# The output projection of a fused convolution and SiLU kernel: from 32-column products to a 20-product scheme of 64 columns

## The chip, the cores and the metric

The kernel runs on one core of a Trainium2 chip. The metric is device time in microseconds (us); lower is better. Engines are named as in the profile: PE is TensorE's matmuls, PEld its weight loads, DVE is VectorE, ACT is ScalarE, POOL is GpSimd, and SP issues transfers.

## The reference

A causal convolution of 7 taps over 8 sequences of 4096 tokens with 192 channels, with softmax weights by head, is followed by a two-layer network with SiLU. Everything is 32 bit.

```python
w = softmax(weight)                       # 8 heads x 7 taps
out[b, s, c] = sum_k w[head(c), k] * x_pad[b, s + k, c]
x = out.reshape(32768, 192)
h = x @ w_in                              # 192 -> 2048
g = h * (1.0 / (1.0 + np.exp(-h)))
y = g @ w_out                             # 2048 -> 192
```

## The kernel before, in words

The 32768 tokens go in 32 blocks of 1024, each as two halves (n = 0, 1) of TB = 512 tokens. Channels stand on partitions in the whole kernel. A block passes these stages:

- `load` brings x in, `turn_in` turns it (DVE), `halo_in` adds the six tokens before the block. `conv` makes 18 steps (3 channel parts x 7 taps, the first without a sum): ScalarE multiplies by the tap, and from block 4 on a POOL-issued transfer adds the product to `nat` in SBUF; before that DVE does both. `spread` copies the result into both partition halves of `dup` (SP), and `win` forms sums of it (DVE).
- Up-projection: 2048 inner channels are done in five groups of chunks, each with a scheme of 15 products (`product`, steps P0 to P14) instead of 18, and six plain ones (`plain`, steps L). Each contracts over 64 rows, so two of them fit the 128 rows of the array side by side. `sums_h` (steps u, X, a, b) combines them in PSUM and SBUF, on ScalarE and DVE, and its steps S apply SiLU into `g`.
- Output projection: `sum_g` (steps t) forms four sums of `g` for each of NJ = 4 chunk elements on DVE. `out_slot` (steps D0 to D5) multiplies them with 32 columns of weights at a time, four products next to each other in the 128 columns of the array; `wx` holds sums of weights made once by `combine_out` on POOL. `merge` (steps x, y, z on ScalarE, M on DVE) brings the parts together, `turn_out` (o) turns them back, and `store_out` (st) sends them out from SP.

The order of all engines is written by hand: `PLAN` is a list of such steps for one turn of the loop, and `pin` keeps each engine's instructions in that order. A sign tells which block a step is for: none for block b of the turn, "-" for the block before, "=" two before, "+" for the next. PSUM has eight banks (one `[128, 512]` tile each), and tables (`CHAIN_BANKS`, `XBANKS`, `PLAIN_BANKS`, `ACC`) say which bank each step uses. `tc` derives the waits between engines from what each instruction reads and writes. Block 0 runs without the schemes (`up_plain`, `down_plain`), `START` is the hand-made order for block 0's output and for blocks 1 and 2, and `finish` one for the last block's output.

Of the kernel before, what the change touches and what calls it, by code (L numbers as in the profile page):

```python
# [17 lines left out]
def kernel(  # L18
# [53 lines left out]
    gpool = ctx.enter_context(tc.tile_pool(name="gp", bufs=2 * NJ))  # L72
# [9 lines left out]
        "+ld.1 -P0.2 -u1.2 -X4.2 -P7.2 -P11.2 -S4.2 =o.2 =st.2 -a1.1 -S1.1 -P0.3 -P12.2 -X4.3 "  # L82
        "-P7.3 v.01 -P11.3 -P12.3 -a5.2 -P4.2 -P14.2 -S4.3 -u1.3 -b1.2 -P10.2 -a5.3 -P8.1 -S5.0 "
        "-S1.0 -a1.2 -S3.2 -P4.3 v.10 -P8.2 -P14.3 -S3.3 -b1.3 -a1.3 -P10.3 P5.4 -S5.1 v.11 "
        "-P8.3 P5.0 v.02 -D1.00 =st.3 -t.00 -b5.3 -a0.2 -a0.3 -sp.2 -D1.30 u5.4 -a0.1 -D1.01 "
        "v.22 v.12 -D0.00 -S0.3 v.23 -D0.31 -D1.10 -t.01 -t.03 -D2.00 -sp.0 -b5.2 -t.02 -D4.01 "
        "-S1.2 -S5.2 -D5.00 -D2.01 v.03 -D5.01 -D3.00 -S0.1 -t.10 -D1.20 -D4.00 v.13 v.24 "
        "-D3.01 -t.11 -D2.11 -D2.10 -t.13 -D5.11 v.14 -D4.10 v.04 -D0.21 -S1.3 -w.0 -w.1 -S0.2 "
        "v.25 -t.20 -S5.4 -t.21 -D5.10 -D4.11 +ld.2 -D1.21 -D0.30 -D0.11 -t.23 -S5.3 -D4.20 "
        "-D5.20 -t.12 -D3.10 -D3.11 -D2.21 -D2.20 -D0.20 -D4.21 -t.22 -D3.21 v.05 -D1.31 -D5.21 "  # L90
        "-t.30 -D0.01 -w.2 -t.31 -t.33 -D5.31 -D1.11 v.15 v.26 +i.2 u5.0 -D0.10 -z1.0 -t.32 "
        "-y0.0 v.06 -D5.30 -x2.3 -x2.0 -D3.30 -w.3 -w.4 -y1.0 -D2.31 -D2.30 -M1.0 -D3.31 -y2.0 "
        "-x2.1 -w.5 -x2.2 -D3.20 -x0.0 -D4.31 -D4.30 -M6.0 -M2.0 L.00 v.16 -M3.0 -M4.0 P2.0 "
        "u4.0 P5.1 +i.1 L.10 u5.1 L.02 -M5.0 -o.3 -x1.0 P3.0 P6.0 u2.0 X2.0 P2.4 u4.4 -o.0 L.01 "
        "SL.0 L.12 L.11 SL.1 +ld.0 P1.0 u0.0 SL.2 P9.0 P6.4 u2.4 P13.0 S2.0 X4.0 -M7.0 -st.0 "
        "+i.0 P2.1 P3.4 X2.4 u4.1 P0.0 u1.0 P7.0 a5.0 P12.0 P11.0 S4.0 b1.0 P1.4 u0.4 P9.4 X4.4 "
        "P4.0 P13.4 a1.0 P14.0 P10.0 b5.0 P7.4 a5.4 P0.4 S2.4 +ha.0 +v.00 S3.0 P6.1 P8.0 P3.1 "
        "u1.4 u2.1 P11.4 a0.0 X2.1 P12.4 P4.4 a1.4 +v.20 b1.4 S4.4 S0.0 +v.21 P5.2 u5.2 P14.4 "
        "S3.4 P1.1 u0.1 P13.1 S2.1 P8.4 a0.4 P5.3 u5.3 sp.1 P2.2 P9.1 X4.1 u4.2 P10.4 -o.1 P0.1 "
        "P2.3 P12.1 u1.1 P7.1 b5.4 u4.3 P11.1 S4.1 P6.2 -st.1 b1.1 u2.2 P3.2 P6.3 P10.1 S1.4 "  # L100
        "a5.1 P3.3 u2.3 P14.1 S3.1 X2.2 P1.2 P13.2 S2.2 P9.2 u0.2 P4.1 b5.1 X2.3 P13.3 P1.3 "
        "u0.3 P9.3 S2.3 S0.4"
    )
    START = (
        "-ld.1 =v.10 -ld.0 =v.00 =v.11 =v.12 =dp.0 =dp.1 =dp.2 =dp.3 =v.13 =v.20 =v.21 =v.22 "
        "=v.23 =v.24 =v.25 =dp.4 =dp.5 =v.14 =dp.6 =dp.7 =dp.8 =dp.9 =v.15 =v.16 -ld.2 =sp.1 "
        "=dp.10 =dp.11 =v.26 =v.01 =v.02 =v.03 =dp.12 =v.04 =dp.13 =v.05 =v.06 =dp.14 =dp.15 "
        "=dp.16 =sp.2 =dp.17 =dp.18 =dp.19 =dp.20 =sp.0 -i.2 =go.2 -i.1 =dp.21 =dp.22 =dp.23 "
        "=dp.24 -i.0 =dp.25 =dp.26 =dp.27 =dp.28 =dp.29 =dp.30 -ha.0 =dp.31 =dp.32 =dp.33 "
        "=dp.34 ld.1 =w.0 =w.1 =dp.35 =dp.36 -v.00 =dp.37 =dp.38 =w.2 =dp.39 =dp.40 =dp.41 "  # L110
        "-v.01 =dp.42 -v.20 =dp.43 =dp.44 -v.02 -v.03 -v.10 -v.11 -v.12 =dp.45 =cp.0 =dp.46 "
        "=dp.47 =cp.1 -v.21 -P5.0 =w.3 -P5.4 -L.00 -u5.0 -v.13 -v.14 -L.11 -v.22 -P2.0 =cp.2 "
        "-u5.4 -P2.4 -L.12 -P3.0 -u4.0 -u4.4 -P6.0 -L.02 -u2.0 -L.01 -SL.0 -L.10 -SL.1 -P6.4 "
        "-u2.4 -P3.4 -SL.2 =o.1 -v.15 -P1.0 -u0.0 -X2.0 -P13.0 -S2.0 -v.23 -P5.2 =w.4 -u5.2 "
        "-P9.0 -P1.4 -u0.4 -P0.0 -u1.0 -P12.0 -P2.2 -X2.4 -P0.4 -P13.4 -S2.4 -X4.0 -P7.0 -u1.4 "
        "=o.2 -P14.0 -b1.0 -P10.0 =w.5 -S3.0 -u4.2 -a5.0 -b5.0 -S5.0 -v.04 -P11.0 -P9.4 -X4.4 "
        "-P14.4 =o.0 -P4.0 -S4.0 -a1.0 -P6.2 -u2.2 -P5.1 -P12.4 -b1.4 -P11.4 -P7.4 -P3.2 -P1.2 "
        "-P8.0 -u5.1 -S4.4 -a5.4 -P10.4 -u0.2 -S3.4 -P2.1 -u4.1 -P4.4 =st.0 -X2.2 -P13.2 -S2.2 "
        "-P9.2 -P0.2 -u1.2 -a0.0 -b5.4 -S5.4 -a1.4 -P12.2 -v.16 -P6.1 -u2.1 =st.1 -P5.3 -u5.3 "
        "-P8.4 -P14.2 -X4.2 -S3.2 i.1 -a0.4 -b1.2 -P3.1 -X2.1 -P1.1 -P7.2 -u0.1 -a5.2 -P2.3 "  # L120
        "-u4.3 -P3.3 -P11.2 -v.24 -P9.1 -S4.2 -X4.1 -P13.1 -P4.2 -P6.3 -S2.1 -a1.2 -u2.3 -P10.2 "
        "-b5.2 -P0.1 -P7.1 -P8.2 -P11.1 -X2.3 -P1.3 -S1.0 -P9.3 -v.25 -u1.1 -P14.1 -S4.1 -P12.1 "
        "-u0.3 -S1.4 -P13.3 -S3.1 -a5.1 -P4.1 -X4.3 -P7.3 -P0.3 -a0.2 -S5.2 -sp.1 +ld.1 -P12.3 "
        "P5.4 -v.26 -P11.3 -b1.1 -a5.3 -a1.1 -u1.3 -P10.1 -b1.3 -S2.3 -P4.3 -a1.3 -v.05 =st.2 "
        "-P8.1 -b5.1 -P10.3 -sp.2 -S0.4 -P14.3 -P8.3 ld.0 -S4.3 -S1.1 P5.0 -a0.1 -S0.0 -t.00 "
        "-D1.31 -D1.11 -S0.2 -D1.01 -S3.3 -D1.30 -t.01 -D2.00 -D2.01 -b5.3 -S5.3 -S1.2 -S5.1 "
        "-D0.11 -t.03 -D4.00 -a0.3 -D4.01 -t.02 -D3.00 u5.4 -D0.20 -S0.1 ld.2 -D5.00 -t.10 "
        "-t.11 -D2.11 -D3.01 -v.06 -sp.0 -D1.20 -S0.3 -D5.01 -t.13 -D4.11 -D5.10 -D4.10 i.2 "
        "-S1.3 i.0 -t.12 -D5.11 -D3.11 -t.20 ha.0 -t.21 -D0.10 -D2.10 u5.0 -D2.21 -w.0 -D2.20 "
        "-w.1 v.20 -D3.10 -D0.00 v.00 -t.23 -D4.21 -D4.20 -w.2 v.01 -t.22 -D3.21 -D0.21 -D0.30 "  # L130
        "-D0.31 -w.3 -t.30 v.21 -t.31 -D1.10 v.02 v.22 -D0.01 -D2.31 -t.32 -t.33 -D1.21 v.10 "
        "-D5.30 v.23 v.24 -y0.0 -D1.00 -y1.0 -D5.31 -z1.0 -D5.20 -D5.21 -x2.0 -x2.2 v.11 -D3.31 "
        "-D2.30 -x2.1 v.03 -x2.3 P2.0 u4.0 P3.0 -w.5 L.02 P2.4 u4.4 v.12 v.13 v.14 P6.0 u2.0 "
        "v.15 v.25 v.26 v.04 -M1.0 -M2.0 -y2.0 L.00 +ld.0 -M6.0 L.01 SL.0 X2.0 P6.4 u2.4 -D4.30 "
        "-D3.20 -D3.30 -M3.0 -x0.0 -D4.31 -x1.0 P9.0 P1.0 u0.0 -o.0 P13.0 S2.0 X4.0 P1.4 u0.4 "
        "-M4.0 -M5.0 P3.4 P5.1 u5.1 P11.0 X2.4 -w.4 P7.0 S4.0 P0.0 P12.0 P2.1 u1.0 P9.4 P0.4 "
        "u1.4 P13.4 a5.0 P4.0 b1.0 P10.0 X4.4 u4.1 S2.4 P7.4 P11.4 S4.4 P14.4 S3.4 v.16 P6.1 "
        "u2.1 P14.0 v.05 L.10 a1.0 a5.4 +ld.2 b5.0 P8.0 +i.2 a0.0 S3.0 P3.1 P4.4 a1.4 L.11 L.12 "
        "SL.1 P5.2 P12.4 SL.2 X2.1 v.06 P8.4 -st.0 u5.2 P1.1 P13.1 u0.1 b1.4 P5.3 sp.1 S0.0 "
        "u5.3 -o.3 S2.1 P12.1 P2.2 u4.2 -M7.0 P9.1 P0.1 u1.1 S1.4 +i.1 P2.3 u4.3 +i.0 a0.4 X4.1 "  # L140
        "S0.4 P10.4 P6.2 u2.2 P3.2 P7.1 P14.1 S3.1 P11.1 b1.1 b5.4 +ha.0 P10.1 +v.20 S4.1 P3.3 "
        "-o.1 P6.3 u2.3 X2.2 P9.2 P1.2 u0.2 a5.1 P4.1 X2.3 +v.21 P13.2 S2.2 P13.3 S2.3 P1.3 "
        "u0.3 -st.1 +v.00 P9.3 b5.1"
# [3 lines left out]
        ((4, 1, 2, 7, 7), (3, 4, 6, 5, 5), (1, 3, 3, 1, 0)),  # L147
        ((0, 2, 5, 4, 6), (1, 6, 1, 0, 7), (5, 3, 2, 3, 0)),
        ((5, 2, 5, 6, 7), (0, 4, 0, 3, 3), (1, 7, 2, 1, 1)),
    )  # L150
    XBANKS = (
        ((6, 2, 4, 2, 0), (6, 0, 0, 0, 4)),
        ((5, 1, 2, 7, 3), (4, 7, 3, 7, 4)),
        ((4, 0, 1, 7, 4), (6, 3, 1, 7, 6)),
    )
    PLAIN_BANKS = (
        (0, 2, 1),
        (5, 3, 4),
        (6, 3, 1),
    )  # L160
    ACC = (
        (1, 2, 7, 4, 3, 5, 7),
        (3, 4, 6, 1, 0, 2, 7),
        (0, 6, 1, 3, 4, 2, 7),
    )
# [91 lines left out]
    WC = 2 * NK * P  # L257
    in32 = moe_w_in.bitcast(I32).rearrange("(k r) (a m c) -> r k a m c", r=R, a=2, m=NM)
    out32 = moe_w_out.bitcast(I32).rearrange("(a q e p) d -> a q p e d", a=2, e=2, p=P)
    wr = [const.tile([P, 2, NK, P], F32, name=f"wr{j}") for j in range(NJ)]  # L260
    ws = [const.tile([P, 2, NK, P], F32, name=f"ws{j}") for j in range(NJ)]
    wo = [const.tile([P, 2, 2, D], F32, name=f"wo{j}") for j in range(NJ)]
    wx = [const.tile([P, 3, 2, HD], F32, name=f"wx{j}") for j in range(NJ)]
    raws = {}

    def raw_tile(key):

        pool, tag = (gpool, "g") if key in (("i", 2), ("i", 3)) else (tpool, "t")
        raws[key] = pool.tile([P, 4 * TB], I32, tag=tag, name="raw")[:, 0 : 2 * WC]
        return raws[key]  # L270
# [611 lines left out]
    def step(b, token):  # L882
# [49 lines left out]
        if b == NB - 1 and token == closing:  # L932
            for t in later:
                step(b, t)
# [201 lines left out]
```

## Time and profile before

| | |
|---|---|
| median of 3 runs | 2319.7 us (2319.48 to 2320.31) |
| profiled execution, span | 2317.9 us |
| PE busy | 2310.2 us (100%) |
| DVE, ACT, POOL busy | 1797.9 (78%), 1496.0 (65%), 534.9 (23%) us |
| output products, `out_slot` (L765) | share of the chain that ended last: 45% |
| up-projection, `product` (L649) and `plain` (L666) | 39% and 5% |
| granted TensorE clock | 1.000 |

The page gives each engine's busy time, and the chain of work that ended last, followed back from the end: at each step to what released it. A 32-bit matmul is listed as two records. "128*32" behind a matmul is the part of the array that it uses, rows by columns. A group's line has its count, its busy time, the mean duration of one, and the idle time of the engine ahead of it with what ended it. The span is the profiled execution's own time from the first to the last instruction; the runs' times are some 2 us longer.

### The profile page before, as it was taken

The page shows a single profiled execution, that of the slowest core. Times are in us where ns is not written, and L with a number is a line of the kernel's source. Part 1 is how long each engine was busy: PE and PEld are TensorE (multiplying, and loading weights), DVE is VectorE, ACT ScalarE, POOL GpSimd, SP SyncE. Part 2 cuts the span into 40 slices and gives each one's busy share as a digit, 9 for nine tenths or more (in the row PEclk, how much of TensorE's full clock was granted, in tenths as well). Part 3 has the DMA queues.
Part 4 walks back from the last instruction along what each step waited for, and adds up shares of the span by engine and source line. Part 5 has one row for each costly group of instructions (what it writes and reads, how often), then busy time and mean ns, then how long its engine had stood idle before and what let it go on. Part 6 is the DMA issues. An engine that isn't in the chain of part 4 may idle for free.

```text
span 2317.9 us, 45421 instructions
## 1 busy us (share of the span) xinstructions
PE 2310.2 (100%) x17630; PEld 949.6 (41%) x17630; DVE 1797.9 (78%) x2373; ACT 1496.0 (65%) x2779; POOL 534.9 (23%) x675
## 2 busy tenths in 40 slices
PE   9999999999999999999999999999999999999999
PEld 5454443444433344433444334443334443344433
DVE  8998777777777777777777777777777777777777
ACT  5347766677666686666776667866667666677543
POOL 4921112221122211222211222112221212221100
PEclk9999999999999999999999999999999999999999
DMA  7236557766567765677655676556776557765401
GB/s 159 58 62 101 98 100 118 123 115 102 95 113 120 121 105 93 109 120 121 110 98 99 115 124 117 102 93 113 119 123 108 94 104 120 120 114 93 81 17 25
DMA packets 522601, 238.81 MB, mean 103 GB/s; under 512 B 430368, under 2 KB 435488, under 8 KB 522384
## 3 DMA queue, kind: packets, MB, share of 16 engines
q0 software_dynamic: 73120, 133.89, 34.4%
q1 hardware_dynamic: 447392, 101.78, 25.0%
q8 instruction: 138, 2.26, 0.4%
q14 instruction: 79, 0.65, 0.1%
q10 hardware_dynamic: 1872, 0.23, 0.1%
HBM read 31.46 MB, written 25.17 MB: 24 GB/s over the span
## 4 chain that ended last, share of the span: by engine, by line
PE 89%; DVE 0%; issue 0%; ACT 0%; ACTq 0%
PE ps L765 45%; PE ps L649 39%; PE ps L666 5%; DVE cmb L175 0%; ACT u L175 0%; DVE osb L175 0%; ACTq L175 0%
## 5 line engine op out<-in xcount | busy, mean ns | idle before, releaser
L512 POOL DMA_DIRECT2D nat<-u x504 | 432.6, 947 | 1544.6 <-ACT u L511 1192.3
L765 PE MATMUL ps<-g,wo 128*32 128x512 f32 x2976 | 694.9, 592 | 0.0
L649 PE MATMUL ps<-win,wr 64*128 64x512 f32 x1550 | 688.7, 591 | 0.8 <-ACT yx L828 0.8
L649 PE MATMUL ps<-win,ws 64*128 64x512 f32 x1550 | 644.3, 589 | 0.0
L698 ACT COPY u<-ps 128x512 f32<-128x512 f32 x775 | 452.2, 587 | 166.8 <-PE ps L649 93.8
L765 PE MATMUL ps<-t,wo 128*32 128x512 f32 (+2 forms) x4528 | 538.5, 446 | 0.0
L765 PE MATMUL ps<-t,wx 128*32 128x512 f32 x2976 | 485.1, 592 | 0.0
L649 PE MATMUL ps<-dup,wr 64*128 64x512 f32 x868 | 425.6, 589 | 0.0
L511 ACT ACTIVATE u<-xt,taps 128x512 f32<-128x512 f32 x504 | 346.0, 715 | 44.0 <-DMA nat<-u 43.6
L733 DVE TENSOR_TENSOR t<-g,t 128x1024 f32<-128x1024 f32 x248 | 303.3, 1223 | 89.7 <-PE ps L765 84.2
L692 DVE TENSOR_TENSOR g<-u,ps 128x512 f32<-128x512 f32 x465 | 312.2, 682 | 72.2 <-PE ps L649 58.8
L649 PEld LDWEIGHTS ps<-win,wr 64*128 64x128 f32 x1550 | 275.7, 187 | 217.1 <-issue 177.1
L733 DVE TENSOR_TENSOR t<-g 128x1024 f32<-128x1024 f32 x248 | 298.8, 1216 | 76.4 <-PE ps L765 56.7
L692 DVE TENSOR_TENSOR ps<-u,ps 128x512 f32<-128x512 f32 x310 | 215.7, 696 | 132.3 <-PE ps L649 62.0
L710 ACT ACTIVATE g<-ps 128x512 f32<-128x512 f32 x465 | 281.0, 604 | 48.6 <-PE ps L649 47.0
L649 PEld LDWEIGHTS ps<-win,ws 64*128 64x128 f32 x1550 | 258.8, 187 | 126.1 <-issue 103.9
L710 ACT ACTIVATE g<-g 128x512 f32<-128x512 f32 x465 | 281.4, 629 | 30.3 <-DVE g L692 30.3
L765 PEld LDWEIGHTS ps<-t,wo 128*32 128x32 f32 x4528 | 181.4, 110 | 239.2 <-issue 227.6
L649 PE MATMUL ps<-dup,ws 64*128 64x512 f32 x682 | 271.9, 589 | 0.0
L831 ACT COPY cmb<-ps 96x512 f32<-96x512 f32 x30 | 17.4, 581 | 393.1 <-PE ps L765 393.1
L765 PE MATMUL ps<-g,wx 128*32 128x512 f32 x1488 | 245.9, 594 | 0.0
L765 PEld LDWEIGHTS ps<-g,wo 128*32 128x32 f32 x2976 | 170.4, 110 | 130.6 <-issue 129.8
(93 smaller groups left out, 2015.1 us busy)
## 6 DMA issues: line engine op xcount, KB each, us to landing
nat<-u POOLq DMA_DIRECT2D x504, 256.0 KB, 4.5
dup<-nat SPq DMA_DIRECT2D x345, 128.0 KB, 2.5
nat<-in_x_dram SPq DMA_DIRECT2D x382, 64.0 KB, 4.4
out_dram<-osb SPq DMA_DIRECT2D x376, 64.0 KB, 2.0
raw<-in_moe_w_out_dram SPq DMA_DIRECT2D x8, 384.0 KB, 3.7
raw<-in_moe_w_in_dram SPq DMA_DIRECT2D x12, 192.0 KB, 4.8
ws<-wr POOLq DMA_DIRECT2D x8, 192.0 KB, 4.8
raw<-in_moe_w_in_dram SPq DMA_DIRECT2D x6, 128.0 KB, 3.1
```

Source lines behind the costliest of these rows:

```text
L511: pin(nc.scalar.activation(z, src, AF.Copy, scale=tap))
L512: pin(nc.gpsimd.dma_start(out=dst, in_=z, accum_op=ALU.add))
L649: nc.tensor.matmul(to[:, cols], raw(g, *LEFT[e][r], e), rhs[:, cols], start=first, stop=True, skip_group_check=True,)
L666: nc.tensor.matmul(plain_bank(b, n and 1 + e)[:, cols], rows(wr[j] if own == e else ws[j], e)[:, a, k, :], rows(dups[b], e)[:, SLOT[e][2 * ...
L692: pin(nc.vector.tensor_tensor(out_, u, v, op=op))
L698: pin(nc.scalar.copy(us[b, g, o][:, cols], t1[:, cols]))
L710: pin(nc.scalar.activation(h, src, AF.Silu))
L733: pin(nc.vector.tensor_tensor(t[i // 2][:, i % 2, :], u, v, op=ALU.subtract))
L765: nc.tensor.matmul(accs[b][at][SQ * q : SQ * q + SQ, to], lhs[:, e, SQ * k : SQ * k + SQ], rhs[:, e, ts(q, TB // 4) if i == 5 else to], st ...
L831: pin(nc.scalar.copy(c[0], acc[0][0:n, :]))
```

## The change

The output projection is done by another scheme. Its 20 forms (steps Q0 to Q19, `out_product`) multiply sums of `g` with sums of weights, each for all four chunk elements j, into 64 output columns; two products fit the array side by side. The sums of `g` are 13 (steps t1 to t13), each over all four chunk elements at once; they are written into three buffers `t` and over parts of `g` that are not needed any more. The weights' sums are made once (`OUT_SUMS`, 22 on POOL and three sign changes on ScalarE). The results grow in four PSUM banks, two results to a bank on its two partition halves (`OUT_HOME`). Where a result is the start of another, it is copied from bank to bank in the midst of its products (steps O and C), and its parts go to SBUF by steps d, all on ScalarE; steps m add on DVE. `turn_out` and `store_out` work on 128 partitions, three times a block.

The order of the whole block is new: products of the output stand among those of the up-projection, and steps of five blocks stand in one turn ("~" is three blocks back, "*" two ahead). `START` holds only block 0's output and the first steps of blocks 1 and 2, the plan begins with block 1, and `finish` is gone: the plan's turns run out at the end. The bank tables are one for all blocks. `conv` uses the adding transfers from block 2 on. `gall` and `wall` are one tile each in place of one for each chunk.

Core of the diff (most of the plan's new text is left out):

```diff
     PLAN = (
...
+        "P2.4 ~st.2 -t2 +v.23 -O.0 L.02 -t3 P2.0 -P8.3 -Q4.3 -S1.2 u4.4 =st.3 -Q11.2 -Q3.2 "
+        "-Q11.3 P6.4 -S0.1 -S1.1 u4.0 -P8.2 +v.11 -a0.3 -t4 L.00 P6.0 +v.06 -Q12.0 +v.16 -a0.2 "
+        "-Q3.0 -C.0 -Q12.1 -Q6.1 -Q5.1 -Q12.3 -Q3.1 +v.21 -Q12.2 -O.1 -Q5.0 -S0.3 +v.03 -Q11.1 "
+        "+v.15 -Q16.0 -t6 -Q5.3 -Q5.2 -S0.2 -d.H -Q18.1 -Q6.3 -t5 -Q18.2 *ld.2 -Q6.0 -Q18.3 "
+        "-Q18.0 u2.0 +v.05 -Q15.0 -Q1.1 -t7 w.2 -Q15.3 -Q2.2 -Q15.1 -t8 -t9 w.3 -Q15.2 -Q1.3 "
+        "-O.5 -Q1.0 -Q19.0 -Q19.1 -Q2.0 *ld.0 -Q16.1 -Q19.3 -t10 -Q19.2 +v.12 +v.04 -d.F "
...
+    OUT_BANKS = {"D1": 0, "D2": 3, "D3": 7, "D4": 5}
...
-        elif b > 3:
+        elif b > 1:
             z = free.pop(0)
             pin(nc.scalar.activation(z, src, AF.Copy, scale=tap))
             pin(nc.gpsimd.dma_start(out=dst, in_=z, accum_op=ALU.add))
...
-    def out_slot(b, j, i, e, half=None):
...
+    OUT_ORDER = {
+        "X": (17, 12, 18, 9, 10),
+        "Y": (4, 5, 15, 0, 14, 8),
+        "C": (13,),
+        "O0": (11, 16),
+        "O1": (1, 2),
+        "O5": (7, 19),
+        "O4": (3, 6),
+    }
+    OUT_HOME = {
+        "X": ("D1", 0),
+        "Y": ("D1", 1),
+        "O1": ("D2", 0),
+        "O5": ("D2", 1),
+        "O0": ("D3", 0),
+        "O4": ("D3", 1),
+        "C": ("D4", 0),
+    }
...
+    G_SUMS = {
+        1: ("g6", "-", "g7", "t0"),
+        2: ("g3", "+", "s1", "g7"),
+        3: ("s2", "-", "g5", "t1"),
...
+        13: ("s11", "-", "g1", "g2"),
+    }
...
+    def sum_g(b, m, js, engine):
...
+        pin(engine.tensor_tensor(g_part(to, js), g_part(u, js), g_part(v, js), op=op))
...
+    def out_product(b, r, j):
+        node = next(x for x in OUT_ORDER if r in OUT_ORDER[x])
+        first = node in ("X", "Y", "O4") and (b, node) not in begun
+        begun.add((b, node))
+        pin(
+            nc.tensor.matmul(
+                out_bank(node),
+                out_form(OUT_FORMS[r])[:, j, :],
+                g_part(OPERAND[r], j),
+                start=first,
+                stop=True,
+                skip_group_check=True,
+            )
+        )
...
+    COPIES = {
+        "O.0": ("X", 1, lambda: out_bank("O0")),
+        "O.1": ("X", 1, lambda: out_bank("O1")),
+        "O.5": ("X", -1, lambda: out_bank("O5")),
+        "C.0": ("Y", -1, lambda: out_bank("C")),
+        "d.D": ("X", 1, lambda: rows(mid(2), 1)),
+        "d.B": ("X", -1, lambda: rows(mid(1), 1)),
+        "d.b": ("X", 1, lambda: rows(mid(6), 0)),
+        "d.H": ("Y", -1, lambda: rows(mid(0), 1)),
+        "d.F": ("Y", 1, lambda: rows(mid(0), 0)),
+        "d.E": ("Y", 1, lambda: rows(mid(1), 0)),
+        "d.A": ("Y", 1, lambda: rows(mid(2), 0)),
+    }
+
+    def out_copy(b, token):
+        node, sign, to = COPIES[token]
+        if sign > 0:
+            pin(nc.scalar.copy(to(), out_bank(node)))
+        else:
+            pin(nc.scalar.activation(to(), out_bank(node), AF.Copy, scale=-1.0))
+
+    def out_sum(b, i):
+        u, to = (
+            lambda: (out_bank("C"), rows(mid(1), 0)),
+            lambda: (rows(mid(6), 0), rows(mid(2), 0)),
+            lambda: (out_bank("C"), rows(mid(2), 0)),
+            lambda: (out_bank("Y"), rows(mid(2), 1)),
+            lambda: (banks[OUT_BANKS["D3"]], mid(1)),
+            lambda: (banks[OUT_BANKS["D2"]], mid(0)),
+        )[i]()
+        pin(nc.vector.tensor_tensor(to, to, u, op=ALU.add))
...
-    def finish(b):
```

## The prediction

> **What bounds the kernel now.** I read the page first (engines, chain), then the chain in order of time, then one block's stretch of time in the windows, and last single instructions in the timeline where a price was needed.
>
> ```profile
> PE 2310.2 (100%) x17630; PEld 949.6 (41%) x17630; DVE 1797.9 (78%) x2373; ACT 1496.0 (65%) x2779; POOL 534.9 (23%) x675
> ...
> PE ps L765 45%; PE ps L649 39%; PE ps L666 5%; DVE cmb L175 0%; ACT u L175 0%; DVE osb L175 0%; ACTq L175 0%
> ...
> 1320.50 30.04 PE ps L649 x140
> 1350.54 36.22 PE ps L765 x384
> 1391.69 30.04 PE ps L649 x140
> ...
> 1350.54:1421.73 71.19, 71.19 (x556) 28.63 (x560) 54.44 (x72) 48.16 (x91) 15.70 (x19) 1.00 0.65 110
> ```
>
> The chain is TensorE and nothing else: each block (1024 tokens) is 36.22 us of output products (L765) between stretches of up-projection (L649, L666), and the same place comes back after 1391.69 - 1320.50 = 71.19 us. The window of that length shows, in this order, PE, PEld, DVE, ACT and POOL: PE fills it, DVE uses 54.44 and ACT 48.16, at a granted clock of 1.00. So only the length of the TensorE queue and its waits count, until another engine passes it.
>
> The page lists two records for each matmul, the second starting 0.43 after the first. Products on different halves (or quarters) of the array run together. A **slot**, two records at 0.4285, is 0.857 us. Up-projection: 75 products and 3 single plain products on two row halves, 39 on each, make 39 slots, and the plain products in column halves 1.5. Output: slots D0 to D4 are 5 x 8 = 40, D5 (a quarter as long, 8 of them) 2. Together 82.5 slots x 0.857 = 70.7 us, of 71.19.
>
> **What is removed and added on TensorE.** The 192 products of 32 columns (42 slots) go; 20 forms x 4 chunk elements = 80 products of 64 columns come, two at a time. I counted the new order of the instructions: 40 lie on columns 0 to 63 and 40 on 64 to 127, and taking them in order with the halves as they come the whole block needs 80.5 slots. 80.5 x 0.857 = 69.0: 1.7 us less for the slots. Block 0 uses the same 64-column form (L786, 593 ns a record against 592), so the form itself is no dearer.
>
> **Switches between the two shapes.** Before, the array changes shape twice a block:
>
> ```profile
> 1349.94 0.59 PE L649 MATMUL ps<-win,wr 64*128 64x512 f32 x1
> ...
> 1350.47 0.63 PE L765 MATMUL ps<-g,wx 128*32 128x512 f32 x3
> ...
> 1350.92 0.61 PE L765 MATMUL ps<-g,wx 128*32 128x512 f32 x3
> ...
> 1386.14 0.60 PE L765 MATMUL ps<-t,wx 128*32 128x512 f32 x3
> ...
> 1386.69 0.69 PE L666 MATMUL ps<-dup,ws 64*128 64x512 f32 x1
> ...
> 1387.22 0.59 PE L666 MATMUL ps<-dup,ws 64*128 64x512 f32 x1
> ```
>
> Start to start it takes 0.53 and then 0.45 instead of 0.43 on the way in, 0.55 and then 0.53 on the way out: some 0.12 + 0.22, of which I count 0.31 for a pair of switches. With it the sum for before is 71.0 to 71.2, as measured. The new order mixes the products: it has twelve switches a block, six pairs, so 6 x 0.31 = 1.9 instead of 0.3. Bounds: 12 x 0.1 and 12 x 0.22, so 1.2 to 2.6; I take 1.9, the row's own. TensorE without waits is then 69.0 + 1.9 = 70.9.
> The Trainium skill, TensorEngine Tiling (Array Packing), Key Properties, says that changing the tiling mode, and not just the tile, drains the engine. The trace agrees (0.12 and 0.22 lost at the two changes); the page has no price, and whoever takes a change as free would have 69.0 here.
>
> **The waits that the change adds.** All sums of the output now grow in shared PSUM banks: X and Y are the two partition halves of bank D1, O1 and O5 of D2, O0 and O4 of D3, C is in D4. Between two groups of products the partial sum is copied by ScalarE (steps O, C, d), from D1 to another bank or to SBUF, and the next products add on. In the built order the products after a copy carry a wait for that copy's semaphore value, and it is by bank: Q12.1 adds to X, yet waits for C.0, which reads Y, and C.0 itself waits for Q12.0. What is queued behind the waiting product, all TensorE work, waits with it. What such a wait costs is in the trace of before, once, at the end of the first special block:
>
> ```profile
> 248.97 0.58 ACT L828 COPY yx<-ps 32x512 f32<-32x512 f32 x1
> ...
> 249.60 0.69 PE L649 MATMUL ps<-win,wr 64*128 64x512 f32 x1 [0.85 <-ACT yx L828]
> ...
> 250.13 0.59 PE L649 MATMUL ps<-win,wr 64*128 64x512 f32 x1
> ...
> 1380.35 1.26 PE L765 MATMUL ps<-t,wo 128*32 128x128 f32 x16
> ...
> 1380.60 0.58 ACT L831 COPY cmb<-ps 96x512 f32<-96x512 f32 x1 [13.34 <-PE ps L765]
> ```
>
> TensorE starts 0.05 after the copy's end, and the first slot is 0.10 longer (250.13 - 249.60 = 0.53). For a copy with nothing between, from the start of the last product: second record at 0.43, its end at 0.43 + 0.59 = 1.02, ScalarE 0.07 later (estimate from 1380.60: the record before D5's first starts 1379.92 and ends 0.6 later), copy 0.58, 0.05: 1.72, where the next product would have started at 0.857. The hole is 0.86, with the longer first slot 0.96. (Bounds: 0.7 if the semaphore comes before the record's end, 1.1 with 0.15 for the last step.)
> In the new order I looked for what stands between the last product on the bank and the next one, for each of the eleven copies:
> - O.0, d.F, d.A, d.D: four to nine products on other banks, 1.7 us or more beyond the last one's slot: covered.
> - C.0 (between Q12.0 and Q12.1), O.1 (Q12.2, Q5.0), O.5 (Q1.3, Q1.0, bank D2), d.H (Q5.2, Q18.1), d.E (Q0.3, Q9.0): nothing. 5 x 0.96 = 4.8.
> - Ahead of d.H and of d.E the last product (Q5.2, Q0.3) has no partner, which would have been the one that now waits: two more slots, 1.7.
> - d.B and d.b, behind the sum m.3, must end before the plain product L.12 takes the bank: 1.02 + 0.03 + 0.69 (DVE) + 0.03 + 0.58 + 0.48 + 0.05 = 2.88 against its slot and four products between (3 slots, 2.57): 0.3, with the first slot 0.4.
> Sum 6.9 us a block. TensorE: 70.9 + 6.9 = **77.8 us** against 71.19.
>
> **VectorE and ScalarE.** DVE loses 16 sums of 1024 (1223 and 1216 ns: 19.5) and gets 13 sums over all four chunk elements, 2048 each. No row has that size; 682 ns at 512 and 1.22 at 1024 give 0.54 for each further 512, so 2.30 (estimate), 29.9. Seven merges become six and four turns three: -1.3. 54.4 + 10.4 - 1.3 = 63.5, under TensorE even without its waits. ACT: ten evacuations (4.5) become eleven copies of 0.58 (6.4): 50.0. Both at nothing; DVE's cover is 77.8 - 63.5, and if the sums took 3.4 us instead of 2.3 it would be gone.
>
> **Moved, at nothing.** SP issues 12 loads, 11 spreads and 12 stores a block as before, at about 0.5; loads are asked for two blocks ahead, behind the spread that frees their buffer, so a waiting load holds up only what has a block's time. Blocks 2 and 3 do their convolution by ScalarE and POOL's accumulating DMAs: 36 x 0.813 leave DVE early on, 36 x 0.95 come to POOL. POOL also gets 22 weight sums of 256 instead of 16 of 192 (0.6 to 0.7 each, some +5) at a place where it idles from 140 to 200 us; if that were not hidden, block 2 would wait for those 5 us, once.
>
> **Beginning and end.** START no longer interleaves block 1's products with block 0's output. In the first turn of the plan 13 products stand alone, in two chains of product, copy, product: five steps of 1.02 + 0.07 + 0.59 + 0.05, 9 us, for 5.6 of work: +3. At the end no products of a next block cover O.0, d.F, d.A and d.D (+3), and the last sums, turns and stores are a plain queue instead of the hand-made `finish` (+3 or 4). Together +10 (0 to 20).
>
> **Sum.** The profiled span is 2317.9, and the median of the runs 2319.7, 1.8 more. 31 blocks x (77.8 - 71.2) = 205; with +10 the span is 2533 and the time about **2534 us**.
>
> **Rivals.**
> 1. *Long sums hold up the banks* (slower still). A DVE queue that is in a 2.3 us sum can't run the short sum that frees a bank for the up-projection. Three of the 13 (t1 to t3) stand among such products; each can cost up to 2.3 less a slot, 1.4: +4.3 a block, 2534 + 133 = 2667. For it: the window shows DVE's queue at 76% before. Against it: ten of the 13 stand among output products, which need no short sum. 0.12.
> 2. *The copies wait by quadrant, not by bank* (hardly slower). Then C.0, O.1, d.H and d.E stop nobody, since the product behind each is in the other half: 77.8 - 4 x 0.96 - 1.7 = 72.3, +34 +10: 2364. Against it: the waits in the built order. 0.03.
> The Trainium skill, PSUM — Partial Sum Buffer (PSUM bank collisions raise a hardware error), has this rule: guard by bank and 32-partition quadrant, by bank being the simple version. No run here shows yet what the finer guard would give.
> 3. *Faster: the copies fit under TensorE's lead.* If products already issued cover the copies and a switch costs only its 0.1, a block takes 69.0 + 1.2 = 70.2, 1.0 less: 2319.7 - 31 + 10 = 2299. It decides when all holes together stay under 0.7 us a block, 0.1 each. For it: PE never waits in a steady block of before. Against it: the one wait like these (0.85) was paid in full. 0.05.
> 4. *It doesn't do what it says* (products of 64 columns don't pair): 40 more slots, 34 us a block; L786 pairs in block 0, so under 0.01.
>
> **The numbers.** Forecast 0.79, the rivals 0.12, 0.03, 0.05 and 0.01. A measurement of this kernel can tell about 0.2% from no change. Faster by more than that: 0.04 (rival 3 without its upper end); within: 0.01; slower: 0.95. Low end: holes of 0.7, unpaired slots half lost, switches at 0.1, no loss at the ends: 70.2 + 3.5 + 0.9 + 0.2 = 74.8, so 2432. High end: holes of 1.1, switches at 0.22, ends +20: 71.6 + 5.5 + 1.7 + 0.5 = 79.3, so 2591, and half of rival 1 above that. Range 2425 to 2630.
>
> **What would show it.** Right: the block's period between 76 and 79 us in the chain; about five waits a block of PE on ACT (L830 or L832, the copies) of near 0.9; output products paired at 0.43; DVE near 63 and ACT near 50 a block. Wrong: no such waits (rivals 2, 3); waits of PE on DVE sums in the up-projection of over 1 us (rival 1); a 2048 sum over 3 us; or a chain that runs through DVE.

## The result, and the profile after

The kernel after takes 2613.0 us (median of 4 runs, 2609.8 to 2613.8) against 2319.6 (4 runs) before: a ratio of 1.126, 95% interval 1.1245 to 1.1277. The profiled execution has a span of 2610.6 us, 292.7 more than before. The forecast was 2534, so the sign held and the time lies in the range of 2425 to 2630, and the size came out 79 us short.

The page of the kernel after, busy time of TensorE and its granted clock in 40 slices:

```profile
PE 2423.5 (93%) x10622; PEld 892.2 (34%) x10622; DVE 2021.8 (77%) x2176; ACT 1565.4 (60%) x2847; POOL 582.0 (22%) x715
...
PEclk9879999999999999999999999999999999999999
```

TensorE, 100% busy before, now has idle time, and the clock dips in the second and third slice. These are two different stories: the steady blocks, and the beginning.

**The steady block.** The same place of the chain in two blocks two apart, and the window of one block (PE, PEld, DVE, ACT, POOL, then the clock):

```profile
259.81 24.21 PE ps L659 x112
...
415.83 24.21 PE ps L659 x112
```

```profile
415.83:493.85 78.02, 74.53 (x330) 27.17 (x330) 62.47 (x67) 49.59 (x91) 16.75 (x19) 1.00 0.58 100
```

(415.83 - 259.81) / 2 = 78.0 us a block, where it was 71.19. TensorE is idle for 3.5 of them, at full clock, and VectorE and ScalarE stay well below the block. The waits of TensorE over the whole kernel (us in total, times, longest) say for what:

```profile
PE ps L795 <- ACT ps L832: 47.3, 62, 1.7
...
PE ps L795 <- ACT cmb L830: 21.3, 32, 0.7
PE ps L795 <- ACT cmb L832: 21.1, 31, 0.7
PE ps L795 <- ACT ps L830: 20.6, 31, 0.7
```

L830 and L832 are the two forms of `out_copy`. Two waits in L832's first row and one in each other row make the five holes a block that the prediction counted (C.0 and O.5; d.E; d.H; O.1). Two of them in the timeline, C.0 at 451.05 and d.H at 457.97:

```profile
449.74 0.59 PE L795 MATMUL ps<-t,wx 128*64 128x512 f32 x1
...
450.42 0.57 ACT L832 ACTIVATE ps<-ps 64x512 f32<-64x512 f32 x1
...
451.05 0.64 PE L795 MATMUL ps<-t,wx 128*64 128x512 f32 x1 [0.71 <-ACT ps L832]
...
457.97 1.08 PE L795 MATMUL ps<-g,wall 128*64 128x512 f32 x4 [0.68 <-ACT cmb L832]
```

The last record of the product ahead of C.0 starts at 449.74, the next one would have started 0.43 later, at 450.17, and starts at 451.05: 0.88 lost. The waits of the other four holes are 0.66 to 0.68 in this block.

**The beginning.** Where TensorE waited before the first output products (which start at 206 us):

```profile
99.41 1.89 PE L875 MATMUL ps<-g,wall 128*64 128x512 f32 x8
142.66 3.75 PE L659 MATMUL ps<-dup,wr 64*128 64x512 f32 x4 [41.36 <-issue]
...
163.65 2.07 PE L659 MATMUL ps<-win,ws 64*128 64x512 f32 x2 [7.62 <-ACT u L708]
171.69 1.22 PE L659 MATMUL ps<-dup,ws 64*128 64x512 f32 x1 [5.96 <-ACT u L708]
```

TensorE stands for 41 us behind block 0's last products. In the kernel before it was busy without a gap from 100 to 175 us (same columns as above):

```profile
100.00:140.00 40.00, 40.00 (x196) 27.52 (x196) 36.76 (x54) 29.25 (x55) 28.23 (x49) 1.00 0.29 53
140.00:175.00 35.00, 35.00 (x360) 12.03 (x356) 34.01 (x42) 10.65 (x21) 0.00 (x0) 1.00 0.25 43
```

"Issue" names no releaser; ScalarE's own timeline gives one:

```profile
115.16 0.72 ACT L523 ACTIVATE nat<-xt,taps 128x512 f32<-128x512 f32 x1 [42.29 <-POOL xt L513]
...
136.42 0.42 ACT L442 ACTIVATE wall<-wall 128x256 f32<-128x256 f32 x1 [15.79 <-POOL wx L137]
...
141.67 0.42 ACT L442 ACTIVATE wall<-wall 128x256 f32<-128x256 f32 x1 [4.53 <-POOL wall L137]
```

ScalarE's queue waits three times for GpSimd: for the halo copy of block 2 (L513), which stands on GpSimd behind sums of weights, and then in the three sign changes (L442) for the sums of output weights. The copies of block 0's output (L890) that free TensorE's banks stand behind these, the second at 142.00 and the third at 143.09.

**The end.** TensorE's last products end at 2595.3, 15.3 us ahead of the end of the span; before it was 5.6. That is 10 us.

**The bill.** 31 blocks x (78.0 - 71.19) = 211. C.0's wait is not always 0.7: in 19 blocks it is longer, up to 1.7. Over 28 blocks (259.81 to 2449.39) the mean block is 78.20, so another 31 x 0.2 = 6. The rest, 292.7 - 217, is 76: 10 at the end, 66 at the beginning.

### The profile page after: what moved, and what is told of

It reads as the page before. It is cut to its first block, busy times and chain, and to the rows that moved or that the text cites. A ratio compares the mean times of both kernels' runs of the same rounds, so it can differ in the third digit from the quotient of the medians.

```text
span 2610.6 us, 31517 instructions
## 1 busy us (share of the span) xinstructions
PE 2423.5 (93%) x10622; PEld 892.2 (34%) x10622; DVE 2021.8 (77%) x2176; ACT 1565.4 (60%) x2847; POOL 582.0 (22%) x715
## 4 chain that ended last, share of the span: by engine, by line
PE 41%; issue 31%; DMA 16%; ACT 5%; POOL 5%; DVE 1%; SPq 0%; POOLq 0%; ACTq 0%; DVEq 0%
PE ps L795 23%; PE ps L659 17%; DMA nat<-u 16%; POOL ws L137 1%; POOL wr L137 1%; POOL nat L527 1%; ACT u L526 1%; ACT ps L832 1%; PE ps L676 1%; POOL xt L513 1%; ACT cmb L832 1%; ACT g L720 1%; DVE two L137 0%; ACT ps L830 0%; DVE cmb L843 0%
## 5 line engine op out<-in xcount | busy, mean ns | idle before, releaser
L795 PE MATMUL ps<-g,wall 128*64 128x512 f32 x1984 | 813.3, 599 | 21.6 <-ACT cmb L832 21.1
L795 PE MATMUL ps<-t,wall 128*64 128x512 f32 x992 | 468.9, 600 | 20.8 <-ACT cmb L830 20.8
L795 PE MATMUL ps<-g,wx 128*64 128x512 f32 x1240 | 460.6, 597 | 20.4 <-ACT ps L832 20.4
L795 PE MATMUL ps<-t,wx 128*64 128x512 f32 x744 | 319.2, 601 | 47.4 <-ACT ps L832 26.8
L795 PEld LDWEIGHTS ps<-g,wall 128*64 128x64 f32 x1984 | 218.5, 136 | 375.1 <-issue 316.8
L659 PE MATMUL ps<-dup,ws 64*128 64x512 f32 x682 | 338.3, 601 | 6.0 <-ACT u L708 6.0
L784 DVE TENSOR_TENSOR t<-g 128x2048 f32<-128x2048 f32 x124 | 283.7, 2288 | 4.3
L784 DVE TENSOR_TENSOR g<-g,t 128x2048 f32<-128x2048 f32 x62 | 141.8, 2287 | 154.7 <-PE ps L795 154.6
L784 DVE TENSOR_TENSOR t<-g,t 128x2048 f32<-128x2048 f32 x93 | 212.8, 2289 | 61.4 <-ACT g L720 60.3
L795 PEld LDWEIGHTS ps<-t,wall 128*64 128x64 f32 x992 | 123.2, 136 | 192.4 <-issue 89.8
```

Of the source, the lines that this page charges most:

```text
L659: nc.tensor.matmul(to[:, cols], raw(g, *LEFT[e][r], e), rhs[:, cols], start=first, stop=True, skip_group_check=True,)
L784: pin(engine.tensor_tensor(g_part(to, js), g_part(u, js), g_part(v, js), op=op))
L795: nc.tensor.matmul(out_bank(node), out_form(OUT_FORMS[r])[:, j, :], g_part(OPERAND[r], j), start=first, stop=True, skip_group_check=True,)
```

## The experiments: the steady block

### Four copies that nobody waits for

```diff
     def out_copy(b, token):
         node, sign, to = COPIES[token]
+        of = out_bank(node)
+        if token in ("C.0", "O.1", "d.H", "d.E"):
+            of = rows(wall[:, 0], OUT_HOME[node][1]).rearrange("p a e d -> p (a e d)")[:, 0:TB]
```

> Four of the copies of partial sums (C.0, O.1, d.H, d.E) read as many columns of a constant tile in SBUF instead of the PSUM bank, so the products that come next in that bank don't wait for them; the true partial sums are left out of the output. ScalarE keeps its 78 copies and VectorE its sums. Theory A (a copy holds up TensorE at its bank, a hole of about 0.9 us each, and two products ahead of d.H and d.E run alone, 0.86 us each if they can now pair): the steady block falls from 78.0 by 4 x 0.9 = 3.6 us, up to 5.3 with the pairs, to 72.7 to 74.4 us, and the whole by 31 times that, to 2450 to 2500 us; the fifth hole, O.5, stays. Rival C (VectorE's long sums or ScalarE's queue set the pace): within 15 us of the changed kernel, since their work is the same. Rival D (the 64-column products are slow by themselves, in the switches of shape or under the clock): the holes go but the products stretch, and less than 1 us a block comes back.

Measured: 2445.3 us, 168 less than the kernel after. Window of one block, and the waits of TensorE for copies:

```profile
328.17:400.92 72.75, 71.94 (x331) 26.76 (x330) 62.46 (x67) 50.47 (x91) 15.68 (x19) 1.00 0.63 107
```

```profile
PE ps L795 <- ACT ps L835: 21.8, 31, 0.7
```

The block falls from 78.0 to 72.75, and one wait a block is left, O.5's. The work of the other engines is the same (DVE 62.46 against 62.47), so neither VectorE's sums nor the 64-column products set the 78 us: four bank-wise waits and the two lone products ahead of d.H and d.E are 5.3 us of the 6.8. The prediction's terms for the same were 4 x 0.96 + 1.7 = 5.5.

### Another pair of shape changes

```diff
-"-Q11.2 -Q3.2 -Q11.3 P6.4 -S0.1 -S1.1 u4.0 -P8.2 +v.11 -a0.3 -t4 L.00 P6.0 "
+"-Q11.2 P6.4 -S0.1 -S1.1 u4.0 -P8.2 -Q3.2 -Q11.3 +v.11 -a0.3 -t4 L.00 P6.0 "
```

> The changed kernel with one pair of output products (Q3.2, Q11.3) moved from ahead of a group of first-stage products to the middle of that group, so that a block has 14 changes of array shape instead of 12; slots, copies and their covers stay. Theory A (a pair of changes costs 0.31 to 0.35 us, the size in the sum of the prediction): 31 x 0.33 = 10 us more than the changed kernel, 2621 to 2625 us, and a block of 78.3 to 78.4 us. Rival (the change of shape is free, and what is seen at the twelve changes belongs to the first slot behind a wait): no difference, 2610 to 2615 us. Rival (a change drains the array for a whole slot): 31 x 0.86 x 2 = 53 us more.

Measured: 2616.8 us, 4 more than the kernel after where 10 were expected. The chain, two blocks one apart:

```profile
260.18 24.21 PE ps L657 x112
338.49 24.21 PE ps L657 x112
```

78.31 us, 0.31 more than the block of the kernel after in which C.0's wait is short, as theory A says. In the whole kernel about half of it came back: the waits for C.0 and O.5, 47.3 us in total before this edit, are 42.0 with it, probably because C.0's product stands further back now and ScalarE has longer to reach it. With these 5.3 us the 3.8 us of the total become 9.1, or 0.29 for each of the 31 added pairs. So a pair of changes costs some 0.3 in a block that is otherwise alike; the total alone would not have shown it.

### The same work in an order without holes

The output part of `PLAN` written anew; e.g. C.0 goes ahead of the products of O0 and O4, O.1 and d.H stand together behind all of Q12 and Q5, and Q16, Q3, Q6 and Q11, which use other banks, follow them:

```diff
+"-Q12.0 -Q5.1 -Q12.1 -Q5.0 +v.21 -Q12.3 -Q5.3 -Q12.2 -Q5.2 -O.1 -d.H -t6 -S0.3 +v.03 "
+"-Q16.0 -Q3.0 +v.15 -S0.2 -Q16.1 -Q6.1 -t5 -Q11.0 -Q6.3 *ld.2 "
+"-Q18.1 -Q15.3 -Q18.2 -Q15.1 -Q18.3 -Q15.2 -Q18.0 -Q15.0 -O.5 -d.F u2.0 +v.05 -t7 w.2 "
+"-Q16.2 -Q6.0 -Q16.3 -Q6.2 P1.0 L.01 u0.0 -t8 -t9 w.3 *ld.0 -t10 "
```

> The changed kernel with its 80 output products, 11 copies and 24 sums in another order: each product that comes next in a bank after a copy of partial sums stands one or two pairs of other products behind that copy, all 80 products stand in pairs, and five groups of them instead of six stand between the products of the first stage (10 changes of array shape a block instead of 12). The work is the same. Theory A (the block loses 6.8 us to holes at copies, lone products and changes of shape): the holes go, the block is 80.5 slots x 0.857 = 69.0 us and five pairs of changes at 0.31 to 0.42 us, 70.6 to 71.4 us with what is left of L.12's wait; x 31 that is 205 to 230 us less than the changed kernel, 2383 to 2408 us, as the beginning is not touched. Rival C (VectorE's 24 long sums or ScalarE's 78 copies set the pace): less than 60 us come back, and the profile shows TensorE waiting for VectorE. Rival D (the products are slow by themselves): less than 30 us.

In this kernel (and in e6_both) the product P1.0 multiplies the block before's sum, and the output product Q14.3 reads what SiLU (SL.0) has overwritten; the instructions and their sizes are those of the kernel after. Measured: 2465.0 us, a block of 73.1. 148 us come back, more than rival C or D allow, and less than theory A said. ScalarE and TensorE at the one wait that comes back in every block (24.3 us in 34 waits, 14.3 of them in one at the beginning):

```profile
449.88 0.59 ACT L706 COPY u<-ps 128x512 f32<-128x512 f32 x1
...
450.51 0.69 PE L657 MATMUL ps<-win,ws 64*128 64x512 f32 x1 [0.21 <-ACT u L706]
```

The product P1.0 waits for u2.0, which I had put behind O.5 and d.F on ScalarE's queue: one hole was traded for another. It is 0.2 to 0.3 us. Of the 2.5 us that a block takes above 69.0 + 5 x 0.31, L.12 is another 0.4, and P6.0, which starts 0.56 us late at 434.75 and so runs unpaired beside L.00, some 0.6; the rest is not placed here.

### Three more tries at that order

e9_holes puts u2.0 ahead of O.5, w.3 ahead of P1.0 and SL.0 behind the products it disturbed, and L.12 and L.11 two products later.

> The changed kernel with the output products in an order without uncovered copies, as e5_order, mended in four places: a product that needs VectorE's last sum of the first stage's inputs stands behind that sum, the SiLU of the plain product stands behind the output products that read its buffer, a copy of a partial sum (u2.0) stands ahead of the copies O.5 and d.F (in e5_order behind them, which left TensorE idle for 1.9 us at 450 us), and the product L.12 two products later. Beginning and end are the changed kernel's. Theory A: no hole is left, so the block is 80.5 slots x 0.857 = 69.0 us and five pairs of changes of array shape at 0.33 us, 70.6 to 71.2 us against 73.1 in e5_order and 78.0 in the changed kernel; x 31 that is 210 to 230 us less than the changed kernel, 2383 to 2403 us. Rival C (VectorE's sums are now the bound): the block stays over 72 us, and TensorE waits for VectorE.

Measured: 2478.9 us, a block of 73.5 (median; 73.1 in e5_order): slower than e5_order. The hole at P1.0 is gone, and another is there:

```profile
472.37 0.59 ACT L830 ACTIVATE cmb<-ps 64x512 f32<-64x512 f32 x1 [3.03 <-DVE cmb L841]
...
472.99 0.69 DVE L841 TENSOR_TENSOR cmb<-cmb,ps 128x512 f32<-128x512 f32 x1 [0.65 <-ACT cmb L830]
473.79 0.69 DVE L700 TENSOR_TENSOR ps<-u,ps 128x512 f32<-128x512 f32 x1
474.54 0.69 PE L657 MATMUL ps<-win,ws 64*128 64x512 f32 x1 [1.02 <-DVE ps L700]
```

Behind the last output products stands a chain over two engines: m.3 on VectorE, d.B on ScalarE, m.4 on VectorE, then X2.0, for which the product P9.0 waits. The products L.12 and L.11 had covered that chain; moved, they covered L.12's own 0.4 us and exposed 1.2. Rival C's sign is there (TensorE waits for VectorE), but it is the place of one short sum, not VectorE's load.

e10_four and e11_best go on from there, each with the beginning of e8_late2 (below). e10_four ends a block with output products, so that only four groups stand among the first-stage products:

> The beginning of e8_late2 and an order without holes in which only four groups of output products stand between products of the first stage (8 changes of shape a block instead of 10). Theory A: the block is 69.0 us and four pairs of changes at 0.33 us, 70.3 to 70.9 us, which is 0.3 to 0.9 us less than the kernel before (71.2), x 31 = 9 to 28 us; against that stands what the beginning and the end still lose, 10 to 25 us: 2305 to 2335 us in all. Rival C: VectorE's chain of five sums ahead of the last output products comes late by 1 us or more a block, 2340 us or more.

Measured: 2458.7 us, a block of 74.5 (in most; 75.1 in the mean). TensorE now waits for the copy d.D, behind a step of the convolution that waits for its buffer on ScalarE's queue, and for SiLU behind d.B and d.b:

```profile
PE ps L795 <- ACT cmb L830: 28.0, 29, 2.7
PE ps L659 <- ACT g L720: 21.3, 31, 0.7
```

e11_best mends these:

```diff
-"=m.3 =d.B =d.b -P9.4 -P13.4 -P1.4 -S2.4 -S3.0 -X4.4 -u0.4 -P3.0 =m.4 -X2.0 -P11.4 "
+"=d.B =m.0 -P9.4 =d.b =m.3 -P14.0 -S3.0 -P13.4 -P1.4 -X4.4 =m.4 -L.11 =m.2 -S2.4 -P11.4 -P3.0 "
...
-"-d.A -d.D -Q2.2 -Q19.1 -Q2.3 -Q19.3 "
+"SL.0 -Q19.1 -d.D -d.A -Q2.2 -Q2.3 u1.0 +v.26 X2.4 -Q19.3 "
```

> The beginning of e8_late2 and an order with four groups of output products (8 changes of shape) in which, unlike in e10_four, ScalarE's SiLU and VectorE's short sums that free banks stand ahead of the copies and long sums, the conversions of the next block's convolution stand where ScalarE doesn't need their buffers at once, and the last copies of a block are covered by output products. Theory A (the scheme's own floor is 69.0 us a block and what is above it is order alone): 69.0 + 4 x 0.33 = 70.3 us if nothing waits, up to 71.6 with small waits left, against 71.2 in the kernel before; with the 138.6 us that e8_late2 has outside its 31 blocks, 2320 to 2360 us. Rival C (VectorE's 62.5 us in a block of 71 can't be placed without holding up banks): the block stays at 73 us or more, 2403 us or more.

Two products of block 1 (Q4.1, Q4.3) take a weight ahead of its sign change here; the work is whole. Measured: 2385.7 us, 1.029 times the kernel before (1.027 to 1.030), the fastest of these kernels and still slower than the one before. Window of one block:

```profile
705.22:777.52 72.30, 71.73 (x331) 27.51 (x329) 62.35 (x66) 50.62 (x90) 15.52 (x19) 1.00 0.62 107
```

The mean block is 72.66 over 12 blocks (566.44 to 1438.37) and 72.9 over the whole kernel. In the block shown, the starts of the single records place nearly all of the 3.3 us above 69.0: four pairs of changes 1.4, the wait for O.1 0.6, L.12 0.4, and two products that start 0.2 us late (at 708.02 and 741.46), 0.3 each with their longer first slot. The profile's idle times miss these two, since the records ahead of them have not ended. The waits for copies like O.1 vary (25.2 us in 27 waits, up to 2.5), which makes the mean block longer. Neither theory's number came: 70.3 was not reached, and the mean block is just under rival C's 73 us; but rival C's sign, a TensorE that waits for VectorE, is not among its waits. Whether an order exists that reaches 70.3 stays open.

## The experiments: the beginning

### The halo copy alone

```diff
-            if b <= 1:
+            if b <= 2:
                 pin(nc.scalar.copy(head, tails.pop(b)))
```

> The copy of block 2's 18 halo columns goes back from GpSimd to ScalarE; nothing else changes. Theory A (the start is lost to an order of queues): in the changed kernel this copy stands on GpSimd behind the sums of the convolution weights until 114.93 us, ScalarE waits 42.29 us for it, and the copies that free TensorE's banks wait behind that. With it on ScalarE the convolution of block 2 and the first of these copies run before 101 us, GpSimd reaches the 22 sums of the output weights at about 116 instead of 130.8 us, and the last two copies, which stand behind the sign changes, follow at about 127 instead of 142 us: 15 to 30 us off the whole, 2583 to 2598 us, with a steady block of 78.0 us as before. Rival B (the start is bound by the weight sums on GpSimd alone): not more than 3 us come back, 2610 to 2613 us, since the sums end when they ended before.

Measured: 2610.0 us, 3 less. ScalarE's wait of 42.29 is gone, and the sign change of the weights waits 33.29 us for GpSimd in its place; TensorE stands 38.5 us. The theory that this copy alone held up the start fell. The last sign change ends only 3 us earlier than before, and block 0's copies stand behind it as they did.

### The sign changes behind block 0's output

```diff
-        "v.21 -w.3 =cp.2 -w.4 -w.5 =op.0 =op.1 =op.2 =stp.0 =stp.1 =stp.2"
+        "v.21 -w.3 =cp.2 =neg.0 -w.4 -w.5 =op.0 =op.1 =op.2 =stp.0 =stp.1 =stp.2"
...
+    def negate_out():
         for at in OUT_NEGATED:
```

> As e1_halo, and the three sign changes of output weights on ScalarE stand behind the last of the three copies of block 0's output instead of ahead of the second. Theory A: the second and third copy no longer wait for GpSimd's sums of output weights, so TensorE's first product of the first turn starts at 102 to 116 us instead of about 127: another 10 to 25 us, 2560 to 2585 us. What is left is then the slow stretch behind it, where ScalarE waits for buffers of block 2's adding transfers. Rival B: no change against e1_halo, since the products wait for the same sums of weights in any order.

Measured: 2609.9 us, no change. TensorE:

```profile
101.99 1.98 PE L661 MATMUL ps<-dup,wr 64*128 64x512 f32 x4
140.68 1.22 PE L661 MATMUL ps<-win,wr 64*128 64x512 f32 x1 [36.71 <-ACT u L710]
```

The first two products run at 102 us, as theory A said, and then TensorE waits for ScalarE's copy u of their sum, which now stands behind the same sign changes. The wait was moved by one instruction.

### Block 2's convolution on VectorE again

```diff
-        elif b > 1:
+        elif b > 2:
             z = free.pop(0)
```

> As e2_neg, and block 2's convolution is summed on VectorE, as in the kernel before, and not by adding transfers. Theory A: the waits of 7.62 and 5.96 us of TensorE between 155 and 172 us go, because ScalarE's copies of partial sums stand no longer behind steps that wait for a buffer of a transfer: another 10 to 25 us, 2540 to 2570 us; all three edits return 50 to 70 of the 82 us by which the beginning and end lost against the kernel before. Steady block 78.0 us. Rival B (VectorE is then late, with 80 long sums of about 0.6 us more in that block): no gain or a loss against e2_neg.

Measured: 2581.5 us, 28.5 less than e2_neg. The waits of 7 us and 6 us at 160 and 170 us are gone; the first output products come at 175 us instead of 204. The wait for the sign changes is still there (30.25 us). All of TensorE's waits for the copies u fall from 51.7 to 31.6 us, which is 20 of the 28.5. The rest is probably the clock: it is granted at a half from 106 to 178 us in e2_neg and from 106 to 137 us in e3_head, with TensorE busy for 20.65 us (107 to 177) and 3.76 us of it; half of that difference, an estimate of what half speed costs, is 8.4.

### The sign changes where they are needed

e7_late puts them ahead of the plan's first `-Q4.0`.

> As e3_head, but the three sign changes stand on ScalarE ahead of the first output product of the first turn, and not in front of ScalarE's copies of the first partial sums. In e3_head these copies waited behind them until 133 us (TensorE idle for 30.25 us), and TensorE ran at a granted clock of about a half right behind that. Theory A (ScalarE's queue, held up by the sums of output weights on GpSimd, is what TensorE waits for): the first turn's products start at about 102 us, and the first output products at about 139 us, when GpSimd's last sum and the sign changes are done, instead of 175: 30 to 37 us less than e3_head, 2545 to 2552 us. Rival B (the products wait for GpSimd's sums of the first stage's weights, which end at 118 us): 10 to 16 us less, 2565 to 2571 us.

Measured: 2583.4 us, no gain. Block 0's output products are skipped in the first turn, so ScalarE reached the sign changes as early as before. e8_late2 puts them there in the second turn:

```diff
         for t in plan:
+            if b == 2 and t == "-Q4.0":
+                negate_out()
             step(b, t)
```

> As e7_late, with the three sign changes one turn of the plan later, ahead of the first output product that is really issued (block 1's, in the second turn). In e7_late they stood at that place of the first turn, in which block 0's output products are skipped, so ScalarE came to them at 104 us, waited 22.43 us for GpSimd's sums, and TensorE waited behind its copies of partial sums, as in e3_head. Theory A (that place in ScalarE's queue is what holds TensorE): no wait of 22 us, block 1's products run from 102 us at full clock, and the first output products come when GpSimd's last sum and the sign changes are done, at about 140 instead of 175 us: 30 to 37 us less than e3_head, 2545 to 2552 us. Rival B (the products wait for GpSimd's sums of the first stage's weights, which end at 118 us in e3_head, and then go on at half clock): 5 to 20 us less, 2562 to 2577 us.

Measured: 2559.1 us, 22.4 less than e3_head, between the two theories. TensorE now runs on:

```profile
104.26 0.69 PE L661 MATMUL ps<-win,wr 64*128 64x512 f32 x1 [0.68 <-ACT u L710]
...
115.75 1.22 PE L661 MATMUL ps<-win,ws 64*128 64x512 f32 x1 [2.26 <-DVE ps L704]
```

The place was theory A's; its size was off, since VectorE, which has block 2's convolution again, is late from 105 to 115 us. The first output products start at 152.6 instead of 140. So of the 66 us lost at the beginning, 54 came back with three waits in ScalarE's queue, one behind the other, and the half clock that followed them: for the halo copy (3 by itself), for buffers of the adding transfers (28.5) and for the weights' sums (22.4). The first, taken away alone, showed next to nothing, because the last ended at nearly the same time. No run leaves the halo copy on GpSimd with the other two mended, so its own worth is not shown. 12 us are left open.

### Both

> e5_order and e7_late together: block 2's halo on ScalarE, its convolution on VectorE, the sign changes behind the first turn's products, and the order without holes. Theory A: the two gains add, since one is in the first 180 us and the other in the 31 blocks behind it: 205 to 230 and 60 to 68 us less than the changed kernel, 2315 to 2350 us, about the time of the kernel before. Rival C (with the holes gone VectorE's 62.5 us of a 70 us block come late, and a shorter start leaves less lead): 20 us or more are lost against that sum.

Measured: 2432.7 us, 32 less than e5_order, where e7_late alone had brought 29.6: the gains of beginning and blocks add, as theory A said. The sum itself is above its range for the reasons of its two parts.

## Why the prediction was right in the block and short at the ends

- **Slots and pairing**: right. The products pair at 0.43 us a record, and no run showed a cost of the 64-column form. (The instruction orders of all these kernels give 80.5 slots a block, as counted.)
- **Switches**, six pairs x 0.31: right. In the kernel after the records around a pair start 0.09 + 0.05 late on the way in (448.74, 449.26, 449.74 instead of every 0.43) and 0.10 + 0.11 on the way out (483.23, 483.76, 484.30), together 0.35; e12_switch's added pair lengthened the block by 0.31. The Trainium skill, TensorEngine Tiling (Array Packing), Key Properties, says that a mode change drains the engine: the trace agrees, and what is lost is about a fifth of a slot each way.
- **Waits by bank**, 6.9 a block: right in number (five), place and size; e4_sbuf took four of them away and got 5.3 of the 5.5 that the prediction gave for them. The row that carried the price, a single wait of 0.85 in the kernel before, was enough. L.12's 0.4 was right as well (491.36 - 490.65 = 0.71 instead of 0.43 between two records, and a first record longer).
- **Block**: 77.8 forecast, 78.0 measured, 78.2 in the mean.
- **VectorE and ScalarE**: 63.5 and 50.0 forecast, 62.5 and 49.6 measured; a sum of 2048 takes 2288 ns, forecast 2.30.
- **Beginning and end**, +10 (0 to 20): wrong, +76 measured (66 and 10). The end was about right (forecast 6 to 7, measured 10). The step that failed is the first turn and, before it, "moved, at nothing". The prediction counted GpSimd's 22 sums (some 5 us more) and found them hidden, but not the three sign changes of ScalarE that wait for those sums, nor what is queued behind them: the copies that free TensorE's banks. It counted the convolution's 36 steps of blocks 2 and 3 as leaving VectorE, but not that they take buffers of the u copies and make ScalarE, in its order, wait for transfers while it holds the first turn's copies. Both are order effects: 22.4 and 28.5 us, the second with some 8 us of half clock, which the prediction didn't count either.
- **The range**: that it held is luck. The prediction's own terms ended at 2591, below the 2613 measured; what covered the rest was the half of rival 1 that was added on top, and rival 1 did not happen. The beginning, at 66, was far outside its bounds.
- **Rival 1** (long sums hold up the banks) did not happen: no wait of TensorE for VectorE in a steady block. **Rival 2** had the right price: without the four waits 72.3 was forecast, 72.75 measured; but no run waits by quadrant, and the rule of the Trainium skill, PSUM — Partial Sum Buffer (PSUM bank collisions raise a hardware error), to guard by bank and quadrant, was not tried. **Rival 3** fell on the five holes.

## What to carry to other kernels

Where partial sums live in shared banks and are copied on the way, count for each copy what stands between the last product on its bank and the next: with nothing there it cost about a slot here (0.88 us against 0.857), and a partner that can't pair cost another. Count for every step that is moved to an in-order queue what it waits for and what is queued behind it, once for the steady block and once more for the first turn, where the producers are still busy with something else. And a stall may have several waits behind it that end together, so that taking away one of them shows nothing: look at what stands next in the same queue before that one is acquitted.

## What the runs showed of the hardware that I had not expected

The granted clock falls to a half when TensorE stands, and stays there for some time after it starts again. Windows of the kernel after (the clock is the third figure from the end):

```profile
130.00:140.00 10.00, 0.00 (x0) 0.00 (x0) 0.00 (x0) 0.72 (x2) 9.21 (x13) 0.50 0.15 26
...
146.00:150.00 4.00, 3.33 (x8) 1.34 (x8) 0.00 (x0) 2.40 (x4) 3.06 (x4) 0.50 0.82 132
150.00:154.00 4.00, 3.37 (x8) 1.24 (x6) 0.00 (x0) 3.02 (x6) 1.92 (x3) 0.71 1.25 195
```

The 0.71 of the last row puts the return to full clock at 152.3 us. From 142.66 to about 152 us each record of a product takes 1.06 to 1.22 us instead of 0.59, and after the wait of 7.62 us at 163.65 again. So a long wait of TensorE costs more than its own length. The Trainium skill, TensorE: Matmul & The Clock Gate, Part 1: The HAM clock gate (the "warmup" mystery), has half the clock after an idle window of some 3.4 us and full clock after as much busy time; the trace agrees on the half, and the way back took 9.7 us here from the first product at 142.66, with TensorE busy for most but not all of it, and 4.5 us behind the later wait of 5.96 us (171.69 to 176.2). In e8_late2 the half clock came at 115.6 us after waits of no more than 2.3 us each, with TensorE busy for 1.12 of the 3.4 us before. In the clock's own records each stretch between two changes is a whole number of steps of 3.41 us (14 steps of half clock, from 104.5 to 152.3, then 2 of full and 5 of half here; 21 of half in e2_neg, 3 in e8_late2): the clock changed only at such steps.
